# Three weight blocks of the fifth strip taken ahead of the third strip's last part, and a narrower last output piece

## The chip, the cores and the metric

The kernel runs on one core of one Trainium2 chip. The metric is device time in microseconds (us), from runs on the chip. "PE" is TensorE, "DVE" VectorE, "ACT" ScalarE, "SP" SyncE; "span" is the time from the first to the last instruction in the trace of one run, about 1.8 us shorter than the device time.

## The reference, cut to what matters

The result mixes two branches over the same input x (2048 tokens of 640 numbers): a state-space scan and a dense layer with gelu, weighted by a sigmoid gate.

```python
# x: (2048, 640)
g = sigmoid((x * gate_w).sum(-1, keepdims=True))
a = ...                                   # scan h = Lam_bar*h + Bu ; 2*Re(C h) + x*Dskip
b = gelu(x @ w1 + b1) @ w2 + b2           # w1: (640, 1728), w2: (1728, 640)
out = g * a + (1 - g) * b                 # bf16
```

## The kernel before

Only two places matter. The first is the start. x @ w1 for the first 512 tokens needs x transposed (`xT`), and its first six column blocks of w1 (`kf` 0 to 5) are accumulated in six PSUM banks, strip by strip: a strip is one block of 128 rows of w1 (`kd` 0 to 4). Because x is turned on PE, 128 tokens at a time, and copied out of PSUM by ACT or DVE, a strip is also cut into parts of 128 tokens.

```python
def strip(kd, t0, t1, first, f0=0, f1=FA):          # FA = 6
    for kf in range(f0, f1):
        ff1_mm(banks[kf], 0, kf, kd, t0, t1, first, 3)   # banks[kf][:, t0:t1] += w1[kd,kf].T @ xT[kd][:, t0:t1]

def part(kd, a):
    strip(kd, a * P, (a + 1) * P, kd == 0)

# ... strips 0 and 1, interleaved with the turning of x ...
part(2, 0)
# ...
turn_rest(3, pA, (nc.scalar, KA + 1, KD), (nc.vector, KA, KA + 1))   # ACT copies kd 3,4; DVE copies kd 2
# ...
part(2, 1)
part(2, 2)
part(2, 3)                                           # needs the DVE copy of turn_rest(3)
# ... two sines on ACT ...
for kf in range(FA):
    # ... (kf == 3: one small matmul, "prmB", for the biases)
    for kd in (4, 3):
        ff1_mm(banks[kf], 0, kf, kd, 0, CH, False, 3)    # CH = 512 tokens
```

Before all this, nine warm-up matmuls on constants run while the first DMAs land. The second place is the end. The last 128 tokens' output leaves in pieces: PE sums a piece, DVE multiplies it by the gate and adds the other branch, and a DMA takes it out.

```python
def cuts(ti):
    return ((0, HD), (HD, 512), (512, D)) if ti == NT - 1 else HALVES      # HD = 320, D = 640

for i, (d0, d1) in enumerate(cuts(ti)):
    # ... ten matmuls into p, then on DVE: ot[:, d0:d1] = p * g + gb[:, d0:d1]
    if ti == NT - 1 and i > 0:
        s0 = 0 if i == 1 else d0                     # the first of the two DMAs carries pieces 0 and 1
        q = nc.sync if i == 1 else nc.scalar
        q.dma_start(out=out2d[ti * P:(ti + 1) * P, s0:d1], in_=ot[:, s0:d1])
```

Of the kernel before, what the change touches and what calls it, by code (L numbers as in the profile page):

```python
# [16 lines left out]
P = 128  # L17
T = 2048
D = 640
F = 1728  # L20
CH = 512
NCH = T // CH
KD = D // P
# [3 lines left out]
NT = T // P  # L27
TPC = CH // P
H = TPC // 2
HT = H * P  # L30
KSA = 2
HD = D // 2
# [9 lines left out]
def kernel(  # L42
# [32 lines left out]
    def bank(dtype=F32):  # L75
        return ps.tile([P, CH * 4 // (4 if dtype == F32 else 2)], dtype, name="bank")
# [140 lines left out]
    def pe(cols):  # L217
        ck.pe += cols / 2400.0 + 0.002
# [45 lines left out]
    def ff1_mm(p, c, kf, kd, t0=0, t1=CH, first=None, last=KD - 1):  # L264
        w, f0 = (w1a, 0) if kf < FA else (w1b, FA) if kf < FB else (w1c, FB)
        w = w[kd][:, (kf - f0) * P:(kf - f0 + 1) * P]
        nc.tensor.matmul(p[:, t0:t1], lhsT=w, rhs=xT[c][:, kd, t0:t1],  # L267
                         start=(kd == 0) if first is None else first, stop=(kd == last), skip_group_check=first is not None)
        pe(t1 - t0)
# [53 lines left out]
    banks = [bank() for _ in range(FA)]  # L323

    def strip(kd, t0, t1, first, f0=0, f1=FA):
        for kf in range(f0, f1):
            ff1_mm(banks[kf], 0, kf, kd, t0, t1, first, 3)
# [26 lines left out]
    def part(kd, a):  # L354
        strip(kd, a * P, (a + 1) * P, kd == 0)
# [28 lines left out]
    nc.vector.tensor_tensor(out=red, in0=u, in1=kk[:], op=ALU.subtract)  # L384
    part(2, 1)
    part(2, 2)
    part(2, 3)
    nc.scalar.activation(out=FSC[:, 0:KS, 0:NP], in_=red, func=ACT.Sin, scale=TWO_PI_M)
    nc.vector.scalar_tensor_tensor(out=ab, in0=red, scalar=-1.0, in1=red, op0=ALU.mult, op1=ALU.max)
    nc.scalar.activation(out=FSC[:, KS:2 * KS, 0:NP], in_=ab, func=ACT.Sin, scale=-TWO_PI_M, bias=halfpi[:])  # L390
    for kf in range(FA):
        if kf == 3:
            nc.tensor.matmul(pA[:, 0:NB], lhsT=prmB[:], rhs=ident[:, 0:NB], start=True, stop=True, skip_group_check=True)  # L393
            nc.vector.tensor_copy(out=colB[:], in_=pA[:, 0:NB])
            for j in range(KD):
                nc.vector.tensor_copy(out=w1c[j][:, n1c - 1:n1c], in_=pA[:, j:j + 1])
        for kd in (4, 3):
            ff1_mm(banks[kf], 0, kf, kd, 0, CH, False, 3)
    for kf in range(FA):
        ff1_act(banks[kf], 0, kf)  # L400
    two_banks = [bank(), bank()]
# [165 lines left out]
    HALVES = ((0, HD), (HD, D))  # L567
    seeded = {}

    def cuts(ti):  # L570
        return ((0, HD), (HD, 512), (512, D)) if ti == NT - 1 else HALVES

    def seed(ti):

        c, a = divmod(ti, TPC)
        seeded[ti] = []
        for d0, d1 in cuts(ti):
            p = bank()
            dve_now(ck.pe, 0.45, lambda: nc.vector.tensor_tensor(out=p[:, 0:d1 - d0], in0=xn[c][:, a, d0:d1], in1=Dbc[:, d0:d1], op=ALU.mult))  # L579
            seeded[ti].append(p)  # L580
# [69 lines left out]
    def fin_a(c, at={}):  # L650
        let_out(0, c)
        for a in range(TPC):
            ti = c * TPC + a
            lo = a * P
            ot = fwork.tile([P, D], BF16, name="ot", bufs=2)
            if a < TPC - 2:
                seed(ti + 2)
            if a in at:
                at[a]()
            for i, (d0, d1) in enumerate(cuts(ti)):  # L660
                p = seeded[ti][i]
                for j in range(2 * KS):
                    CT = CT_re if j < KS else CT_im
                    nc.tensor.matmul(p[:, 0:d1 - d0], lhsT=hs[c][:, j, lo:lo + P], rhs=CT[:, j % KS, d0:d1],  # L664
                                     start=False, stop=(j == 2 * KS - 1), skip_group_check=True)
                    pe(d1 - d0)

                def f():
                    nc.vector.scalar_tensor_tensor(out=ot[:, d0:d1], in0=p[:, 0:d1 - d0], scalar=gcol[:, 0, ti:ti + 1],  # L669
                                                   in1=gbs[ti][:, d0:d1], op0=ALU.mult, op1=ALU.add)  # L670

                dve_now(ck.pe + 0.2, 0.45, f)
                if ti == NT - 1 and i > 0:
                    s0 = 0 if i == 1 else d0
                    q = nc.sync if i == 1 else nc.scalar
                    q.dma_start(out=out2d[ti * P:(ti + 1) * P, s0:d1], in_=ot[:, s0:d1])
            if ti < NT - 1:
                nc.sync.dma_start(out=out2d[ti * P:(ti + 1) * P, :], in_=ot[:])
# [59 lines left out]
```

## Time and profile before

| | before |
|---|---|
| device time, first three runs | 215.34, 215.99, 216.0 us (median 215.99) |
| span of the profiled run | 213.7 us |
| PE busy | 210.0 us, 98% |
| last matmul starts at | 210.73 us |
| from there to the end | 2.95 us |

The page's head, its row of PE in the first part, and the PE and DVE rows of the 40 slices (each digit is the busy share in tenths):

```profile
span 213.7 us, 3596 instructions
...
PE 210.0 (98%) x1407; PEld 126.1 (59%) x1407; DVE 189.0 (88%) x387; ACT 103.2 (48%) x186; POOL 1.0 (0%) x13
...
PE   8999999999999999999999999999999999999994
...
DVE  2689999999998999999999999999999999993153
...
```

PE is busy in every slice but the last. So a change pays only where PE itself has less to do, or waits less, or where the end after the last matmul becomes shorter. The pitch of the matmuls, which is the distance from one start to the next in the trace's records, is 56 ns for 128 columns and 216 ns for 512 in most of the run.

The chain of waits around 9 us (columns: start us, length us, what):

```profile
...
8.68 0.39 ACT xT L242
...
9.10 0.30 DVE xT L240
9.40 0.04 issue
9.45 0.71 PE bank L267 x7
```

ACT copies for 0.39 us, DVE starts its copy only afterwards and takes 0.30 us, and only then does PE go on. From the records, PE's first matmul of the part starts at 9.446 us and was due at 9.154: a hole of 0.292 us. No other hole of this size stands between there and the end.

The end, as the timeline has it (start us, length us, engine, line, what) and as the DMA view has it (the last number is us from issue to landing):

```profile
...
210.43 0.91 DVE L669 SCALAR_TENSOR_TENSOR ot<-bank,gcol,gb 128x192 bf16<-128x192 f32 x2 [0.27 <-PE bank L664]
...
210.87 0.33 SPq L676 DMA_DIRECT2D out_dram<-ot  x1
211.37 0.36 ACTq L676 DMA_DIRECT2D out_dram<-ot  x1
```

```profile
...
out_dram<-ot SPq DMA_DIRECT2D x1, 128.0 KB
out_dram<-ot ACTq DMA_DIRECT2D x1, 32.0 KB, 1.5
```

Piece 1 leaves with piece 0 at 210.87 on SP's queue, the last 128 columns at 211.37 on ACT's; by the records the large DMA landed at 212.54 and the small one at 212.84, and 0.84 us of closing follow.

### The profile page before, as it was taken

To read this page: it belongs to the slowest core of one execution; us is meant where nothing else is said; L and a number is where in the kernel's file an instruction comes from. 1 tells how busy PE (TensorE), PEld (TensorE's weight loads), DVE (VectorE), ACT (ScalarE), POOL (GpSimd) and SP (SyncE) were. 2 spreads that over 40 slices of the span, in tenths; PEclk is the share of its full clock that TensorE was granted. 3 is DMA by queue.
4 is the path that set the end of the run, shared out by engine and by line. 5 is a ranking of instruction groups with operands and counts; after the bars stand their busy time and mean duration, and the time that the engine had idled before them with its cause. 6 is when DMAs were issued, how large, how long until landed. Compare 5 with 4: busy or idle time off the path is not lost.

```text
span 213.7 us, 3596 instructions
## 1 busy us (share of the span) xinstructions
PE 210.0 (98%) x1407; PEld 126.1 (59%) x1407; DVE 189.0 (88%) x387; ACT 103.2 (48%) x186; POOL 1.0 (0%) x13
## 2 busy tenths in 40 slices
PE   8999999999999999999999999999999999999994
PEld 5845444454576644775457777444457687676773
DVE  2689999999998999999999999999999999993153
ACT  3699856675758588203563210455682422305100
POOL 1000000000000000000000000000000000000000
DMA  6859999998000000051000005100000000100011
GB/s 196 236 133 182 228 172 267 337 204 219 1 0 0 3 0 0 17 178 67 0 0 3 0 0 187 61 0 2 3 0 14 0 3 31 61 34 0 0 66 61
DMA packets 31571, 15.84 MB, mean 74 GB/s; under 512 B 22978, under 2 KB 31554, under 8 KB 31554
## 3 DMA queue, kind: packets, MB, share of 16 engines
q1 hardware_dynamic: 30850, 14.99, 28.8%
q10 hardware_dynamic: 704, 0.62, 0.9%
q8 instruction: 11, 0.18, 0.4%
q14 instruction: 6, 0.05, 0.1%
HBM read 7.48 MB, written 2.62 MB: 47 GB/s over the span
## 4 chain that ended last, share of the span: by engine, by line
PE 98%; DVE 0%; ACT 0%; issue 0%
PE bank L605 27%; PE bank L267 26%; PE bank L664 20%; PE bank L546 20%; PE bank L230 1%; PE bank L621 1%; PE bank L293 1%; PE bank L233 1%; ACT xT L242 0%; DVE ot L669 0%; PE bank L358 0%; DVE xT L240 0%; PE bank L283 0%; PE bank L393 0%; PE bank L368 0%
## 5 line engine op out<-in xcount | busy, mean ns | idle before, releaser
L605 PE MATMUL bank<-w_sb,gel 128*128 128x384 bf16 (+1 forms) x416 | 57.9, 299 | 0.0
L605 PEld LDWEIGHTS <-gel 128*128 128x128 bf16 x416 | 40.3, 98 | 17.0 <-issue 0.8
L549 ACT ACTIVATE bu<-bank 128x512 bf16<-128x512 f32 x40 | 23.6, 597 | 37.6 <-PE bank L546 37.6
L272 ACT ACTIVATE gel<-bank,colB 128x512 bf16<-128x512 f32 x52 | 33.9, 692 | 11.1 <-PE bank L267 10.8
L664 PEld LDWEIGHTS <-hs 128*128 128x128 bf16 x330 | 31.7, 98 | 11.6
L500 DVE TENSOR_TENSOR_SCAN g<-r_c,carry,v 128x512 bf16<-128x512 f32 x30 | 37.2, 1269 | 0.0
L613 ACT ACTIVATE gb<-bank,gcol 128x384 f32<-128x384 f32 (+1 forms) x32 | 15.1, 525 | 33.6 <-PE bank L605 16.8
L267 PE MATMUL bank<-xT,w1a 128*128 128x512 bf16 (+1 forms) x174 | 28.1, 315 | 0.1
L664 PE MATMUL bank<-CT_im,hs 128*128 128x320 bf16 (+2 forms) x165 | 27.1, 295 | 0.0
L664 PE MATMUL bank<-CT_re,hs 128*128 128x320 bf16 (+2 forms) x165 | 27.1, 295 | 0.0
L669 DVE SCALAR_TENSOR_TENSOR ot<-bank,gcol,gb 128x320 bf16<-128x320 f32 (+2 forms) x33 | 17.4, 533 | 9.9 <-PE bank L664 9.5
L546 PE MATMUL bank<-xT,BT_re 128*128 128x512 bf16 x100 | 24.8, 379 | 0.0
L546 PE MATMUL bank<-xT,BT_im 128*128 128x512 bf16 x100 | 24.8, 379 | 0.0
L267 PEld LDWEIGHTS <-w1a 128*128 128x128 bf16 x174 | 14.5, 99 | 11.8 <-issue 0.2
L267 PE MATMUL bank<-xT,w1b 128*128 128x512 bf16 x80 | 17.9, 379 | 0.0
L546 PEld LDWEIGHTS <-BT_im 128*128 128x128 bf16 x100 | 9.8, 98 | 11.8
L579 DVE TENSOR_TENSOR bank<-xn,Dbc 128x320 f32<-128x320 bf16 (+2 forms) x33 | 14.5, 481 | 2.3 <-ACT gb L613 2.3
L546 PEld LDWEIGHTS <-BT_re 128*128 128x128 bf16 x100 | 9.6, 98 | 11.0
L481 DVE TENSOR_TENSOR v<-wa,wb 128x512 bf16<-128x512 bf16 x40 | 15.2, 421 | 0.6
L594 ACT ACTIVATE bank<-b2bc 128x384 f32<-128x384 bf16 (+1 forms) x24 | 11.7, 524 | 7.3 <-DVE ot L669 7.3
L481 DVE TENSOR_TENSOR wa<-TCOS,g 128x1024 bf16<-128x1024 bf16 x20 | 13.7, 685 | 0.1
L267 PE MATMUL bank<-xT,w1c 128*128 128x512 bf16 x60 | 13.7, 379 | 0.0
(99 smaller groups left out, 166.1 us busy)
## 6 DMA issues: line engine op xcount, KB each, us to landing
out_dram<-ot SPq DMA_DIRECT2D x15, 160.0 KB, 1.8
w_sb<-in_B_w_dram SPq DMA_DIRECT2D x1, 2080.0 KB
xn<-in_A_x_dram SPq DMA_DIRECT2D x3, 640.0 KB
w1b<-in_B_w_dram SPq DMA_DIRECT2D x5, 128.0 KB, 4.2
w1c<-in_B_w_dram SPq DMA_DIRECT2D x5, 112.0 KB, 4.9
w1a<-in_B_w_dram ACTq DMA_DIRECT2D x2, 192.0 KB, 3.1
w1a<-in_B_w_dram SPq DMA_DIRECT2D x1, 384.0 KB, 3.4
xn<-in_A_x_dram SPq DMA_DIRECT2D x4, 64.0 KB, 3.2
```

Source lines behind the costliest of these rows:

```text
L267: nc.tensor.matmul(p[:, t0:t1], lhsT=w, rhs=xT[c][:, kd, t0:t1], start=(kd == 0) if first is None else first, stop=(kd == last), skip_grou ...
L272: nc.scalar.activation(out=gel[c][:, kf, :], in_=p[:, :], func=ACT.Gelu_apprx_tanh, bias=b1_c[:, kf:kf + 1])
L481: nc.vector.tensor_tensor(out=o, in0=a, in1=b, op=op)
L500: nc.vector.tensor_tensor_scan(s["g"][:, ri, :], r_c[:, ks:ks + 1].to_broadcast([P, CH]), s["v"][:, ri, :], init, ALU.mult, ALU.add)
L546: nc.tensor.matmul(p[:], lhsT=BT[ks >= KSA][:, kd, (ks % KSA if ks < KSA else ks - KSA) * P:][:, 0:P], rhs=xT[c][:, kd, :], start=(kd == 0 ...
L549: nc.scalar.activation(out=bu[:, ri, :], in_=p[:], func=ACT.Identity)
L579: dve_now(ck.pe, 0.45, lambda: nc.vector.tensor_tensor(out=p[:, 0:d1 - d0], in0=xn[c][:, a, d0:d1], in1=Dbc[:, d0:d1], op=ALU.mult))
L594: nc.scalar.activation(out=v, in_=src, func=ACT.Identity)
L605: nc.tensor.matmul(p[:, col:col + d1 - d0], lhsT=gel[c][:, kf, a * P:(a + 1) * P], rhs=w2_sb[:, kf, d0:d1], start=False, stop=False, skip_ ...
L613: nc.scalar.activation(out=gbs[ti][:, d0:d1], in_=p[:, col:col + d1 - d0], func=ACT.Identity, scale=gcol[:, 1, ti:ti + 1])
L664: nc.tensor.matmul(p[:, 0:d1 - d0], lhsT=hs[c][:, j, lo:lo + P], rhs=CT[:, j % KS, d0:d1], start=False, stop=(j == 2 * KS - 1), skip_group ...
L669: nc.vector.scalar_tensor_tensor(out=ot[:, d0:d1], in0=p[:, 0:d1 - d0], scalar=gcol[:, 0, ti:ti + 1], in1=gbs[ti][:, d0:d1], op0=ALU.mult, ...
```

## The change

The intent is twofold. Three matmuls of the fifth strip (256 tokens each, data already there) are put in front of the part that waits, to fill the hole. And the last piece is made 64 columns wide in place of 128, so that less is left to do after PE's last matmul.

```diff
     part(2, 1)
     part(2, 2)
+    AHEAD = 3
+    strip(KD - 1, 0, HT, False, 0, AHEAD)
     part(2, 3)
 ...
         for kd in (4, 3):
-            ff1_mm(banks[kf], 0, kf, kd, 0, CH, False, 3)
+            ff1_mm(banks[kf], 0, kf, kd, HT if kd == 4 and kf < AHEAD else 0, CH, False, 3)
 ...
     def cuts(ti):
-        return ((0, HD), (HD, 512), (512, D)) if ti == NT - 1 else HALVES
+        return ((0, HD), (HD, D - P // 2), (D - P // 2, D)) if ti == NT - 1 else HALVES
```

## The prediction

> **What bounds the kernel now.** TensorE. In the page's first part PE is busy 210.0 of 213.7 us (98%); the view of waits lists no wait of PE on another engine. I compared each matmul's start in the trace with the one before plus its own columns (56 ns for 128, 216 ns for 512, as neighbouring starts show). From 4.6 us on, one hole stands out: the first matmul of the third strip's last part starts at 9.446 us where 9.154 was due, 0.292 us late. The chain of waits names the cause: ACT's copy of xT (0.39 us from 8.68), then DVE's (0.30 us from 9.10), which starts only after ACT's. From 9.45 to 210.7 us PE issues nearly without a hole. The last matmul starts at 210.73; then come DVE (0.35 us), an output DMA of 32 KB (issued 211.37, landed 212.84) and 0.8 us of closing.
>
> **What the change does.**
> 1. Three 256-column matmuls of the fifth strip go in front of that late matmul; three later ones shrink from 512 to 256 columns: the same columns, three instructions more. Starts in the trace fit N/2.4 + 2.5 ns, which is also what the Trainium skill says ("TensorE: Matmul & The Clock Gate", the section on 56 against 53.3 ns); so the three cost 3 x 109 = 0.327 us where they now stand, and 8 ns in all. Their weights landed at 8.39 us, their token blocks were copied by 8.20. So the hole is filled whole: gain 0.292 - 0.008 = 0.284 us.
> 2. Whether it lasts: ACT's first gelu starts at 12.68 whatever PE does (its table load waits for the sine), but the bank it frees is asked for at 14.55. The tightest thing is a DMA: the fifth part of w1b landed at 13.59 (its first share at 10.58), its weight load stood at 13.905 and would stand at 13.62. Margin 0.03 us; in executions where that DMA lags more, part of the gain is eaten.
> 3. The tail: the middle output piece becomes 256 columns in place of 192, the last 64 in place of 128. PE's sum is the same (64 columns take about 30 ns, as the 65-column matmuls do). On the old clock: the middle piece's matmuls end 0.27 us later; DVE needs about 0.485 us (between 0.418 for 192 and 0.551 for 320), to 211.17; its DMA of 144 KB is issued at 211.20 and, at 1.7 us (1.67 for 128 KB, 1.8 for 160 KB), lands at 212.9. The last piece: DVE about 0.285 us to 211.4, landed at 212.85. So what ends last changes from the small DMA to the middle one, and the end moves by 0 to +0.1 us: no gain, perhaps a small loss.
>
> Net: -0.284 + 0.06 = about -0.22 us of 216, or 0.1%: less than the spread of the three runs (215.34 to 216.0). Before's four times, the profiled run (215.48) with them, average 215.7, so I expect about 215.55, range 215.1 to 216.1. Chances: faster by over 2% 0.005, within 2% 0.99, slower 0.005.
>
> **What would show it.** Hole before the third strip's last part under 0.03 us; all of PE after it about 0.28 us earlier; span 213.4 to 213.6; the middle output DMA lands as late as the last one, or later.
>
> **What would make it wrong.** A hole moving to the w1b weight load near 13.6 us; writing a block's halves at different times bringing a wait that I do not see; the clock's release at the start falling elsewhere; the order of DVE's program changing, since the kernel's own schedule clock counts 2 ns more for each matmul added.

## More of the kernel before

The start once more, by stretches of 1 us (columns: from and to, length, then busy time and number of instructions of PE, PE weight load, DVE, ACT, POOL, then granted clock, DMA share, GB/s):

```profile
...
4.00:5.00 1.00, 1.00 (x15) 0.99 (x14) 0.17 (x1) 0.16 (x2) 0.00 (x0) 1.00 1.04 343
5.00:6.00 1.00, 1.00 (x19) 0.89 (x17) 0.42 (x2) 0.44 (x2) 0.00 (x0) 1.00 0.45 127
6.00:7.00 1.00, 1.00 (x23) 1.00 (x21) 0.32 (x2) 0.28 (x1) 0.00 (x0) 1.00 0.91 244
...
```

The number after PE is what to read here: 15, 19 and 23 matmuls at work in three successive microseconds (one that runs over an edge counts on both sides), all with PE "busy" for the whole microsecond.

## The result

| | before | after |
|---|---|---|
| median, 6 runs each | 215.70 us | 216.12 us |
| lowest to highest | 215.33 to 216.21 | 215.99 to 216.24 |
| ratio (after / before), 95% interval | | 1.0019 (1.0001 to 1.0036) |
| span of the profiled run | 213.67 us | 214.21 us |
| the small bias matmul ("prmB"), in the midst of the last two strips, begins at | 11.073 us | 11.336 us |
| from there to the last matmul's start | 199.652 us | 199.678 us |
| from the last matmul's start to the end | 2.949 us | 3.198 us |

A ratio is the mean time of one kernel's runs over that of the other's runs of the same rounds, so it is not quite the ratio of the medians quoted. The sign is the wrong one: 0.22 us less was forecast, and the median is 0.42 us more. The last three lines of the table divide the span of the two profiled runs. The middle of 200 us did not move (0.03 us); the start is 0.26 us later and the end 0.25 us longer. Some traces, this one among them, lack a few matmul records, about one in 140; they show as gaps of exactly one matmul and are not counted as holes.

The page after, the same lines:

```profile
span 214.2 us, 3591 instructions
...
PE 209.9 (98%) x1399; PEld 127.1 (59%) x1410; DVE 188.9 (88%) x387; ACT 103.2 (48%) x186; POOL 1.0 (0%) x13
...
PE   8999999999999999999999999999999999999994
...
DVE  2599999999998999999999999999999999983152
...
```

The chain of waits at the place of the hole:

```profile
...
9.02 0.17 PE bank L233 x3
9.19 1.44 PE bank L267 x22
...
```

The wait for ACT and DVE is gone; PE runs through 22 matmuls. That part of the prediction did come true. Yet the whole is later, and the stretches of the start show why:

```profile
...
4.00:5.00 1.00, 1.00 (x12) 1.00 (x11) 0.08 (x1) 0.01 (x1) 0.00 (x0) 1.00 1.06 354
5.00:6.00 1.00, 1.00 (x12) 1.00 (x11) 0.44 (x2) 0.40 (x2) 0.00 (x0) 1.00 0.52 109
6.00:7.00 1.00, 1.00 (x20) 1.00 (x18) 0.31 (x2) 0.34 (x2) 0.00 (x0) 1.00 0.92 268
...
```

In the microsecond from 5 to 6, PE had 12 matmuls at work where it had had 19. From the records, the pitch of 107 ns for 128 columns lasts until 6.05 us here; in the profile before it ended at 4.58. The change is not executed before 9 us, so it cannot be the direct cause within the run.

The granted clock in these lines misleads: it reads 1.00 at both pitches. In the traces' own clock records, which the page and its views summarize, nothing at all is recorded so early, and a stretch without a record is shown as 1.00. The first record of the run after, of a full clock, begins at 6.03 us, where the pitch falls. The recorded texts call this moment the clock's release. In e1, e2, e3, e4 and m1, told below, it begins at 5.19, 5.27, 3.59, 5.20 and 6.66 us, each within 0.04 us of the end of the slow pitch. (The profiled runs of before and m2 hold no clock record.)

The end after:

```profile
...
210.95 0.68 DVE L671 SCALAR_TENSOR_TENSOR ot<-bank,gcol,gb 128x256 bf16<-128x256 f32 x2 [0.54 <-PE bank L666]
211.47 0.33 SPq L678 DMA_DIRECT2D out_dram<-ot  x1
211.66 0.36 ACTq L678 DMA_DIRECT2D out_dram<-ot  x1
```

```profile
...
out_dram<-ot SPq DMA_DIRECT2D x1, 144.0 KB
out_dram<-ot ACTq DMA_DIRECT2D x1, 16.0 KB, 1.7
```

The small DMA is issued 0.20 us after the large one (before: 0.50), and takes 1.72 us to land (1.7 in the view) where it took 1.47. By the records both land late: 2.20 and 2.37 us after the last matmul's start, against 1.82 and 2.11 before.

### The profile page after: what moved, and what is told of

The parts are those of the page before. It is cut to its first block, busy times and chain, and to the rows that moved or that the text cites. A ratio compares the mean times of both kernels' runs of the same rounds, so it can differ in the third digit from the quotient of the medians.

```text
span 214.2 us, 3591 instructions
## 1 busy us (share of the span) xinstructions
PE 209.9 (98%) x1399; PEld 127.1 (59%) x1410; DVE 188.9 (88%) x387; ACT 103.2 (48%) x186; POOL 1.0 (0%) x13
## 4 chain that ended last, share of the span: by engine, by line
PE 98%; issue 0%; DVE 0%; DVEq 0%
PE bank L607 27%; PE bank L267 27%; PE bank L666 20%; PE bank L548 20%; PE bank L230 1%; PE bank L623 1%; PE bank L293 1%; PE bank L233 1%; DVE ot L671 0%; PE bank L358 0%; DVEq L735 0%; PE bank L283 0%; PE bank L395 0%; PE bank L368 0%
## 5 line engine op out<-in xcount | busy, mean ns | idle before, releaser
L272 ACT ACTIVATE gel<-bank,colB 128x512 bf16<-128x512 f32 x52 | 33.8, 694 | 10.8 <-PE bank L267 10.6
L267 PE MATMUL bank<-xT,w1a 128*128 128x512 bf16 (+2 forms) x173 | 28.4, 317 | 0.2
L267 PEld LDWEIGHTS <-w1a 128*128 128x128 bf16 x177 | 15.3, 102 | 11.4
```

What stands on the lines that cost most here:

```text
L267: nc.tensor.matmul(p[:, t0:t1], lhsT=w, rhs=xT[c][:, kd, t0:t1], start=(kd == 0) if first is None else first, stop=(kd == last), skip_grou ...
L272: nc.scalar.activation(out=gel[c][:, kf, :], in_=p[:, :], func=ACT.Gelu_apprx_tanh, bias=b1_c[:, kf:kf + 1])
```

## The experiments

Theory A was that the change is a sum of a gain of 0.28 us at the hole and a loss of about 0.25 us at the end, and that the rest of the difference is the moment at which PE's pitch falls from 107 to 56 ns, which varies from run to run and has nothing to do with the change. Rival B was that taking blocks ahead makes the start slower. Rival C was that the new end alone costs all of it.

### Without a gate: each part by itself

**e1: blocks ahead, old end.**

```diff
 # against the changed kernel
-        return ((0, HD), (HD, D - P // 2), (D - P // 2, D)) if ti == NT - 1 else HALVES
+        return ((0, HD), (HD, 512), (512, D)) if ti == NT - 1 else HALVES
```

> The three blocks taken ahead, the old last pieces (192 and 128 columns). Theory A (sum: the change itself is -0.28 us for the filled hole and +0.25 us for the tail; what is left of the +0.57 us of the two profiles is the PE clock's release, 4.58 us in the profile before and 6.05 us in the one after, which falls by chance): no hole over 0.03 us at the last part of the third strip, tail from the last matmul's start to the end 2.95 us, span about 213.4 us with an early release and 214.0 with a late one, times in two groups like those of before, on average about 0.28 us (0.13%) faster than before. Rival B (taking blocks ahead itself makes the start slower): every run at 215.9 or more, release at 6 us every time. Rival C (the new tail alone is what costs): as A for the hole, but no run in the upper group.

Measured: 214.96 to 216.1 us, mean 215.34; ratio 0.9980 (0.9955 to 1.0004). No hole, from the last matmul's start to the end 2.94 us, pitch of 107 ns until 5.21 us. One of six runs lies in the upper group (here about 215.9 us and above), so B, and C as I put it, both fall.

**e2: new end alone.**

```diff
 # against the kernel before
-        return ((0, HD), (HD, 512), (512, D)) if ti == NT - 1 else HALVES
+        return ((0, HD), (HD, D - P // 2), (D - P // 2, D)) if ti == NT - 1 else HALVES
```

> The kernel before with the last pieces 256 and 64 columns wide. Theory A: the hole of 0.29 us is there again, the tail is 3.20 us (the small DMA lands 1.7 us after its issue in place of 1.47), so about 0.25 us (0.12%) slower than before on average, in two groups again. Rival B: same time as before. Rival C: all of the loss and more, 0.4 us slower, every run in the upper group.

Measured: 215.84 to 216.65 us, mean 216.25; ratio 1.0022 (0.9999 to 1.0044). The hole (0.291 us) is there; the end takes 3.21 us. The sign is A's; the size is lost in the spread.

**e3: the changed kernel once more.** No edit.

> The changed kernel once more, to see whether it is always in the upper group. Theory A: some runs are near 215.35 (early release) and others near 216.1, ratio to before near 1.000. Rivals B and C: all runs again in 215.9 to 216.3, release of the clock again at about 6 us in the profile.

Measured: 215.34 to 216.28 us, mean 215.88; ratio 1.0009 (0.9987 to 1.0032). In its profiled run the slow pitch ended at about 3.6 us and the span was 213.56, the end again 3.198. So the changed kernel is not always in the upper group.

**e4: blocks ahead, last pieces 224 and 96 columns.**

```diff
 # against the changed kernel
-        return ((0, HD), (HD, D - P // 2), (D - P // 2, D)) if ti == NT - 1 else HALVES
+        return ((0, HD), (HD, 544), (544, D)) if ti == NT - 1 else HALVES
```

> The three blocks ahead, last pieces 224 and 96 columns wide, between the two versions. Theory A: hole filled; tail between 2.95 and 3.20 us, as an estimate 3.0 (middle piece 0.13 us later than with 192 columns, last piece's DVE work 0.03 us shorter); on average 0.2 us faster than before. Rivals B and C: as for the first two.

Measured: 215.35 to 216.32 us, mean 215.79; ratio 1.0000 (0.9976 to 1.0024). The end takes 3.03 us as estimated; the expected 0.2 us is not seen in these six runs, and could not be, with a spread of 1 us. The end grows in order with the narrower last piece: 2.95, 3.03, 3.20 us.

These runs show the parts in the profiles, but not in the times. Put side by side, the profiled runs without a gate divide cleanly. "Pitch" is when the 107 ns ended, "strips" when the bias matmul begins, "end" from the last matmul's start; the middle was 199.65 to 199.68 us in all of them.

| run | blocks ahead | pitch | strips | end | span |
|---|---|---|---|---|---|
| before | no | 4.58 | 11.07 | 2.95 | 213.67 |
| e2 | no | 5.31 | 11.26 | 3.21 | 214.14 |
| e1 | yes | 5.21 | 10.93 | 2.94 | 213.53 |
| e4 | yes | 5.21 | 10.94 | 3.03 | 213.63 |
| after | yes | 6.05 | 11.34 | 3.20 | 214.21 |
| m1 (told below) | yes | 6.69 | 11.64 | 2.96 | 214.25 |

For the four in the table with blocks ahead, "strips" rises by 0.475 us for each us of later pitch (from 10.93 at 5.21 to 11.64 at 6.69, and 11.34 at 6.05 lies on that line): at half the speed, half of the time is lost. On the same line a pitch of 5.31 would give 10.98, and e2, without the blocks ahead, has 11.26: 0.28 us more, the hole. The end depends on the pieces alone. Two more profiled runs, e3 and m2, had their slow pitch end earlier (about 3.6 and 4.13 us); their strips, at 10.68 and 10.57, lie above the line, since with so early a clock PE has longer gaps between matmuls instead (0.37 us between two starts in e3, where its chain of waits shows a copy of x). An early clock therefore gains less and less. Before itself is such a run: with a pitch of 4.58 the line gives 10.63; the hole adds 0.29, and a gap at 4.97 us (0.211 us between two starts where 0.056 was due) that the four do not have adds 0.155, which makes 11.08 (measured: 11.07). In the same way the start of after, 0.26 us later than that of before, is a sum: 0.70 for the later pitch, less 0.155 for this gap, less 0.284 for the hole.

### Behind a gate: the spread taken away

**g1 to g4.** To make the time blind to the pitch, real work was held back until the pitch had surely fallen: PE warms up longer, and the first real matmul needs an identity matrix that DVE hands out only after a chain of additions. Same edit on the kernel before (g1), the changed kernel (g2), blocks ahead with the old end (g3) and the new end alone (g4).

```diff
-    make_identity(nc, ident[:])
+    ident_raw = const.tile([P, P], BF16, name="ident_raw")
+    make_identity(nc, ident_raw[:])
+    gate = const.tile([P, D], F32, name="gate")
 ...
-    for n in (512, 512, 512, 512, 512, 128, 128, 128, 128):
+    nc.vector.memset(gate[:], 0.0)
+    for _ in range(12):
+        nc.vector.tensor_tensor(out=gate[:], in0=gate[:], in1=gate[:], op=ALU.add)
+    nc.vector.tensor_copy(out=ident[:], in_=ident_raw[:])
+    for n in (512,) * 24:
         nc.tensor.matmul(pA[:, 0:n], lhsT=ones(P), rhs=ones(n), start=True, stop=True)
```

> The kernel before, made blind to when the PE clock is released: 24 warm-up matmuls of 512 columns, and the first real matmul held back by a chain of 12 DVE additions (an estimate from additions of 640 f32 columns at 0.83 us in the trace: until about 10 us), so that the clock is free before real work begins. Theory A (the spread of about 1 us between runs of one kernel is the clock's release): all runs within 0.3 us of each other, about 6 us slower than before as a whole. Rival (spread from elsewhere, a DMA landing or the end): the runs spread by about 1 us as they do ungated.

> The changed kernel with the same gate. Theory A: 0.03 to 0.05 us from the gated kernel before (hole -0.28, tail +0.25, three instructions), if the hole keeps its size behind the gate. Rival B or C (the change itself costs 0.2 to 0.4 us): 0.2 to 0.4 us slower than the gated kernel before.

> Gated, the three blocks ahead alone, old tail. Theory A: 0.28 us faster than the gated kernel before, runs within 0.3 us of each other. Rival B: no faster.

> Gated, the new tail alone. Theory A: 0.25 us slower than the gated kernel before (tail 3.20 us in place of 2.95, and 0.03 us more of matmuls). Rival: no slower.

This try failed. The additions came 0.86 us apart, real work began at 12.58 us, PE stood idle 3.7 us (g2) to 4.2 us (g3), and the pitch of 107 ns came back, so it ended by chance again, as early as 15.5 us in g3 and as late as 16.5 us in g2. Ranges: g1 225.42 to 226.71, g2 225.62 to 226.74, g3 225.12 to 225.51, g4 225.58 to 226.15 us. Nothing follows for the sizes; the lower g3 is of A's sign.

**h1 to h4: a shorter gate.** Eight additions and 20 warm-up matmuls in the same edit; h1 is the kernel before, h2 the changed kernel, h3 blocks ahead with the old end, and h4 the changed kernel with the last output in three DMAs:

```diff
 # h4 only
-                if ti == NT - 1 and i > 0:
-                    s0 = 0 if i == 1 else d0
-                    q = nc.sync if i == 1 else nc.scalar
+                if ti == NT - 1:
+                    s0 = d0
+                    q = nc.sync if i < 2 else nc.scalar
```

> Second try of the gate. In the first try PE stood idle 3.8 to 4.2 us before real work, and matmuls of 128 columns were then issued 107 ns apart again, so the release fell by chance once more. Now 8 additions and 20 warm-up matmuls: real work is to begin at 9.14 us (0.86 us per addition less), PE idle 1 to 2.6 us before it. Theory A: every run within 0.2 us of the others, mean clock above 0.995, the hole of 0.29 us at the last part of the third strip is there. Rival: spread of 0.5 us or more.

> The changed kernel behind the second gate. Theory A: hole -0.28, tail +0.25, so 0.01 to 0.06 us faster or the same (within 0.08 us) as the gated kernel before. Rivals: 0.2 us slower or more.

> Three blocks ahead with the old tail behind the second gate. Theory A: 0.28 us faster than the gated kernel before, with a clear interval. Rival B: no faster.

> The changed kernel behind the second gate, with the output of the last tile in three DMAs (320, 256, 64 columns) in place of two (576, 64): the first 320 columns leave as soon as they are ready. In the profile after, the small DMA's packets begin 1.03 us after its issue and among those of the 144 KB DMA issued 0.2 us earlier; before, 0.87 us after. Theory D (the 64-column DMA lands late because it queues behind the large one): the small DMA lands about 1.47 us after issue again, the middle one 1.55 after, tail 2.95 to 3.0 us, about 0.2 us faster than the changed kernel with the same gate. Rival E (rows of 128 bytes take longer to land by themselves): the small DMA still lands 1.7 us after issue, tail 3.15 or more.

Measured: h1 was 220.94, 220.94, 220.93, 220.94 us. A spread of 1 us became 0.01 us. In h2, h3 and h4, four runs of six each stood within 0.04 us, and two lay about 1.5 us higher, with a mean granted clock of 0.992 in place of 0.998 to 1.000. The profiled run of h2 was one of those. Its stretches after the gate, with h1's first (the granted clock is the third number from the end):

```profile
...
9.14:10.80 1.66, 1.50 (x22) 1.27 (x22) 0.58 (x2) 0.56 (x2) 0.00 (x0) 1.00 0.90 256
10.80:14.00 3.20, 3.20 (x60) 3.19 (x59) 2.02 (x8) 1.56 (x6) 0.00 (x0) 1.00 0.81 189
...
```

```profile
...
9.14:10.80 1.66, 1.51 (x22) 1.27 (x22) 0.58 (x2) 0.55 (x2) 0.00 (x0) 1.00 0.91 256
10.80:14.00 3.20, 3.20 (x34) 3.20 (x33) 0.81 (x4) 0.61 (x3) 0.00 (x0) 0.51 0.77 197
...
```

From 10.8 to 14 us h2 was granted half of the clock and had 34 matmuls at work where h1 had 60. PE had stood idle 2.25 us before the gate in h2, 1.10 us in h1. So the runs are compared within their clock group; k1 to k4 below belong in the same table. Real work begins at 9.14 us in all of them.

| gated kernel | runs with the clock kept | mean | against h1 | runs with the clock fallen |
|---|---|---|---|---|
| h1, before | 4 | 220.94 | | none |
| k1, before, again | 2 | 220.95 | +0.01 | 222.51, 222.41 |
| h2, the whole change | 4 | 220.945 | +0.01 | 222.55, 222.39 |
| h3, blocks ahead alone | 4 | 220.67 | -0.27 | 222.23, 222.14 |
| k2, new end alone | 2 | 221.225 | +0.29 | 222.73, 222.71 |
| k3, one block ahead | 3 | 220.85 | -0.09 | 222.29 |
| h4, whole change, three DMAs | 4 | 220.885 | -0.05 | 222.48, 222.32 |
| k4, whole change, DMAs as before | 4 | 220.88 | -0.06 | none |

Within a row no two runs of the kept clock differ by more than 0.05 us, and k1, the same kernel as h1 on another chip with a slightly longer warm-up, agrees within 0.01. This settles it: the whole change is worth nothing (+0.01), the blocks ahead gain 0.27 us, and the sums agree (-0.27 + 0.29 = +0.02). The fallen group tells the same (222.19 on average for h3 against 222.46 for k1). h1 has the hole in its chain of waits, just as the kernel before had it without a gate:

```profile
...
14.18 0.39 ACT xT L248
...
14.59 0.30 DVE xT L246
14.89 0.04 issue
14.94 0.71 PE bank L273 x7
...
```

Theory D, in the expectation of h4, was that the small DMA lands late because it queues behind the large one; E, that rows of 128 bytes take longer to land by themselves. h4 met neither: the small DMA landed 1.56 us after its issue (1.72 without the split; D had said 1.47, E 1.7). It landed 0.16 us earlier after the last matmul's start than in h2 (2.21 against 2.37), but only 0.06 us came back in time, since the closing waits of SP, taken one after the other, now had two more to pass after the DMA that landed last.

**k1 to k4: control and what was left.** The gate with 23 warm-up matmuls, so that PE idles less. k1 is the kernel before, k2 the new end alone. k3 takes one block ahead, with the old end; k4 leaves the changed kernel's arithmetic as it is and gives the DMAs their old columns.

```diff
 # k3, against blocks ahead with the old end
-    AHEAD = 3
+    AHEAD = 1
 # k4, against the changed kernel
-                    s0 = 0 if i == 1 else d0
+                    s0, s1 = (0, 512) if i == 1 else (512, D)
                     q = nc.sync if i == 1 else nc.scalar
-                    q.dma_start(out=out2d[ti * P:(ti + 1) * P, s0:d1], in_=ot[:, s0:d1])
+                    q.dma_start(out=out2d[ti * P:(ti + 1) * P, s0:s1], in_=ot[:, s0:s1])
```

> Control: the kernel before behind the gate with 23 warm-up matmuls in place of 20, so that PE stands idle for 0.2 to 1.5 us before real work and not 2.4 (where the clock had fallen back in some runs and the time was 222.2 us or more). Real work begins at 9.14 us as before. Theory A: 220.94 us in every run, none at 222. Rival: a second group again.

> The new tail alone, same gate. Theory A: the hole of 0.29 us is there, tail 3.20 us, time 221.2 us (0.27 slower than the control). Rival (the loss needs both parts together): within 0.05 us of the control.

> One block ahead in place of three, old tail, same gate. Theory A (the gain is the PE time put into the hole): a hole of 0.18 us is left (0.292 less 0.109), and the time is 220.83 us, 0.11 faster than the control, against 0.27 with three blocks. Rival (what counts is that any work stands there): 0.27 faster.

> The whole change behind the gate, arithmetic of the last tile still 320, 256 and 64 columns, but the two DMAs carry columns 0 to 512 and 512 to 640 as in the kernel before. Theory D (queueing): the small DMA's packets begin about 1.0 us after its issue, landing at 2.25 to 2.3 us after the last matmul's start, little better than 2.37, time 220.88 or more. Theory E (rows of 128 bytes): from the last packet's end to landing 0.35 us in place of 0.45, landing about 0.11 us earlier. If both have a share: landing at 2.22 to 2.27, time 220.82 to 220.87 us.

k1 missed in one respect: two of four runs still fell back to the slow clock. The other two agree with h1. k2 came out at 221.22 and 221.23 where 221.2 was expected. k3 came out at 220.84 to 220.86 where 220.83 was expected, with a hole of 0.18 us left by the records. The chain of waits shows only 0.02 us of issue between the two groups, because the recorded length of the 256-column matmul, 0.27 us against its pitch of 0.109, covers the rest; the starts tell it: 16.356 us where 16.174 was due.

```profile
...
15.56 0.78 PE bank L273 x13
16.34 0.02 issue
16.36 0.60 PE bank L273 x7
...
```

So the gain goes with the PE time that is put into the hole, at about 0.1 us a block.

In k4 the small DMA carries 128 columns again:

```profile
...
out_dram<-ot SPq DMA_DIRECT2D x1, 128.0 KB
out_dram<-ot ACTq DMA_DIRECT2D x1, 32.0 KB, 1.7
```

By the records it lands 1.655 us after its issue, the end takes 3.14 us, and the time is 220.88. Taking the small DMA apart, with the times of its packets in the records:

| | issue to first packet | first to last packet | last packet to landing | sum |
|---|---|---|---|---|
| before: 256-byte rows, 0.50 us after the large DMA | 0.865 | 0.264 | 0.343 | 1.472 |
| after: 128-byte rows, 0.20 us after it | 1.030 | 0.237 | 0.452 | 1.719 |
| k4: 256-byte rows, 0.20 us after it | 0.991 | 0.267 | 0.397 | 1.655 |
| h4: 128-byte rows, 0.20 us after a DMA of 64 KB | 0.873 | 0.224 | 0.462 | 1.559 |

The large DMA carries 128 KB in before and k4, and 144 KB in after. These times hardly vary: over the other profiled runs with the old or the new pieces and DMAs the sum is 1.47 to 1.49 us with the old end and 1.71 to 1.72 with the new one, gated or not.

k4 and before differ in the distance to the large DMA: of the 0.247 us lost, 0.183 go with that distance. The other 0.064 go with the narrower rows and the large DMA's 16 KB more, which no run here parts. By the bounds set beforehand k4 (landed 2.31 us after the last matmul's start, 220.88 us) came out on D's side. By the table, D accounts for about three quarters, and E may have a share in the rest. It is not the mere distance that delays the first packet: at the same 0.20 us it comes 0.873, 0.991 and 1.030 us after the issue behind 64, 128 and 144 KB. That speaks for queueing behind the data. This is in line with what the Trainium skill says in "DMA: Bandwidth & Descriptors", section "Issuing engines are not separate DMA queues", that DMAs from different engines run on the same 16 DMA engines and interleave: a second queue did not keep the small DMA out of the large one's way.

### Without a gate once more

**m1 and m2.** Blocks ahead with the old end, and the changed kernel, both unaltered.

> Three blocks ahead, old tail, no gate, second time. Theory A: spread from about 214.95 to 216.2 with the clock's release, mean near 215.57 (0.27 below the mean of the 44 runs of before so far, 215.84), give or take 0.2 for six runs. Rival (the first result of 215.34 was luck and there is no gain): mean at 215.84 or above.

> The changed kernel a third time, no gate. Theory A: runs from 215.3 to 216.4, mean 215.84 give or take 0.2. Rival (something in the change makes the release late): again nearly all runs at 215.95 or above, mean 216.0 or more.

m1: 215.24 to 216.03 us, mean 215.53; ratio 0.9983 (0.9966 to 1.0000). m2: 215.23 to 216.37 us, mean 215.75; ratio 0.9998 (0.9978 to 1.0017). The profiled run of m1 caught the latest end of the slow pitch, 6.69 us:

```profile
...
5.00:6.00 1.00, 1.00 (x12) 1.00 (x11) 0.44 (x2) 0.40 (x2) 0.00 (x0) 1.00 0.50 130
6.00:7.00 1.00, 1.00 (x15) 1.00 (x13) 0.06 (x1) 0.16 (x1) 0.00 (x0) 1.00 1.00 248
...
```

Twelve and 15 matmuls in those two microseconds, where before had 19 and 23. Over all runs without a gate, before had a mean of 215.82 us (55 runs, 215.15 to 216.47), the changed kernel 215.91 (18 runs), blocks ahead with the old end 215.44 (12 runs), and the new end alone 216.25 (6 runs). The last two lie 0.38 below and 0.43 above before, the gated sizes plus what the clock's chance adds with few runs.

The best version is the blocks ahead with the old end (e1, m1, h3). It beats the kernel before by 0.27 us behind the gate; the change as given does not. 0.27 us is 0.1% of the time.

## Why the prediction was wrong

Point by point, as the prediction put it:

1. *"the hole is filled whole: gain 0.292 - 0.008 = 0.284 us"*. Right. The chain of waits after shows it, and behind the gate the gain is 0.27 us; one block gives 0.09 (0.10 against k1) where 0.11 was computed.
2. *"Whether it lasts ... The tightest thing is a DMA"*. The gain lasted: the middle of the run, 199.65 us, did not change by more than the 0.03 us of the narrower last piece, which moves the last matmul's start. The feared wait on w1b did not show; in the profile after, that part landed at 11.42 us, well ahead.
3. *"The last piece: DVE about 0.285 us to 211.4, landed at 212.85"*, and from it *"the end moves by 0 to +0.1 us"*. This is the step that failed. DVE and both issues came within 0.04 us of what I had computed, once shifted, and the large DMA landed within 0.05 us of it. What I had forecast to end last, the middle DMA, did not: the small one still did. The term that was mis-sized is the small DMA's time to landing: I carried over about 1.45 us from the profile before, where it followed the large DMA by 0.50 us. Now it followed by 0.20 us and took 1.72 us. With it the last landing moves by 2.39 - 2.11 = 0.28 us (0.03 of that is the last matmul's later start), so the +0.06 of the sum should have been about +0.28 (k2 measured +0.29). With this term right, the net of the prediction would have been 0.0, which is what h2 shows.
4. *"Before's four times ... average 215.7, so I expect about 215.55, range 215.1 to 216.1"*. The base was 0.1 us low (55 runs: 215.82), and the range was too narrow for a kernel whose own runs reach from 215.15 to 216.47. I had named the cause under what would make it wrong (*"the clock's release at the start falling elsewhere"*), but had not put it into the range. That spread is shown to be the start's clock: the table of profiled runs, and the gate that brought 1 us down to 0.01. That PE's pitch of 107 ns is half the clock is read from the gated runs, where the profile has 0.51 of the clock beside it, and from the clock records of the ungated ones, whose full clock begins where that pitch ends.

The recorded difference of 0.42 us between the medians is therefore not the effect of the change. The measured effect is 0.0 us. Of the 0.64 us between the forecast of -0.22 and the recorded +0.42, the mis-sized landing accounts for 0.22; the other 0.42 is put down to the clock: all six recorded runs of the changed kernel lie at 215.99 us or above, as runs with a late clock do, though only the profiled one shows its clock. That all six did is not explained: 24 of 55 runs of before lay at 215.95 or above, so if runs were independent, six of six would come about once in 150 times. In 12 later runs of the same program four did. Whether something of the order in which runs are made decides the moment stays open.

## What to carry to other kernels

On a kernel whose PE never waits, an effect of 0.1% can be measured, but not by repeating runs: find what spreads the runs (here the first microseconds of PE's clock), hold real work back until it has passed, and compare there. When the last output is cut narrower to shorten the end, look at how close its DMA comes to the one before it: here a small DMA issued 0.2 us behind one of 128 KB or more took 0.18 to 0.25 us longer to land, although it was on another queue. Test two small changes made together apart from each other; here one gained 0.27 us and the other lost it again.

## What the Trainium skill lacked or had wrong

- "TensorE: Matmul & The Clock Gate", section "What's actually happening": it says that the window is free-running and the number of slow matmuls differs from run to run. The slow pitch ended between about 3.6 and 6.69 us, and in the clock records the complete stretches of full and half clock last 3.413 us or whole multiples of it (6.827, 208.213). It adds the size: up to 1.3 us between runs of one kernel. No page says that a profile's clock records can begin only at the release, so that a view reads 1.00 before it at a pitch of 107 ns.
- Same page, section "HAM oscillation — how this bites in real kernels": it gives the rule of no PE idle gap over about 3.4 us. Here the clock also fell after single idle gaps of 1.74 us (k2), 1.83 us (k3), 2.25 us (h2), 2.27 us (h4) and 2.39 us (h3), each followed by small waits; it held after 0.85 to 1.10 us (k1, k4, h1). In the clock records of those five, the 3.413 us before the fall have PE busy for 1.32 to 1.58 us, so they need not be idle throughout.
- Same page, section "Back-to-back issue gap": it gives about 81 ns per matmul of 128 columns and 131 ns for 512 in a stream of weight loads and matmuls. Such streams here run at 56 and 216 ns, which is the formula that the page gives for a single gap.
- "DMA: Bandwidth & Descriptors", section "Anatomy of one DMA — SWDGE (gpsimd) path", has most of the fixed time in the write receipt, for DMAs issued by GpSimd. The page has no such split for those issued by SP and ACT, only a figure for the first byte. For the small output DMA here, issued by ACT, 0.87 to 1.03 us lie before the first packet, and 0.34 to 0.46 us between the last packet and the landing. No page says how much later a DMA lands when issued 0.2 us behind another (0.18 us here, behind 128 KB), or what narrower rows add to the landing (at most 0.06 us here from 256 to 128 bytes, with 16 KB moved to the other DMA).
